# Attention over two long K/V caches on one core: cache loads of 8 MB in 64 KB runs, worked on in place

## The chip, the cores and the metric

The kernel runs on one core of one Trainium2 chip; the other cores are idle. The metric is the device time of one execution in microseconds (us), as a median over several executions. Repeated executions of the kernel before agree within about 0.1% (the widest set is 828.7 to 830.0 us), so differences of 1 us between medians can be seen. The cache lies in HBM, the chip's main memory; sixteen DMA engines copy it to the on-chip memory. The profile of a run spans from its first to its last instruction and is some 1.8 us shorter than the time.

## The reference

There are two independent problems, A and B, of the same shape: one query row, 32 heads of 128 numbers, a cache of 16,384 keys per head in bfloat16. A attends to all keys, B only to the last 4,096.

```python
def _A_ref(x, k_cache, v_cache, wq, wo):          # x: [1, 1, 512]
    q = (x @ wq)  # -> 32 heads of 128
    scores = einsum("bhqd,bhkd->bhqk", q, k) * (Dh ** -0.5)
    p = softmax(scores); o = einsum("bhqk,bhkd->bhqd", p, v)
    return o.reshape(1, 1, 32 * 128) @ wo
# _B_ref: the same with k, v = k_cache[:, :, -4096:, :], v_cache[:, :, -4096:, :]
# result: concatenate([a, b], axis=-1)
```

The inputs that must be read once: 134 MB each of A's K and V, 34 MB each of B's K and V, and 4 MB each of two `wq` and two `wo`: 352 MB in all. (MB in this text are the units of the profile; the "4 MB" of a load are 4,194,304 bytes.)

## The kernel before

Each partition of on-chip memory holds a stretch of keys of one head. A "unit" is one 4 MB load of K and one of V: one head of A (128 partitions x 128 keys, a contiguous run of 32 KB per partition), or four heads of B (32 partitions each, again 128 keys and 32 KB). K and V have two such buffers each.

```python
def _load_kv(nc, cx, unit, which):
    t = pool.tile([P, unit.keys, DH], BF16, tag=tag, name=tag)     # 128 keys: 32 KB per partition
    ...
    n = len(unit.heads)                                            # A: 1, B: 4
    src = view[unit.heads[0] : unit.heads[0] + n].rearrange("g (i l) d -> i g l d", i=P // n)
    cx.o(nc.sync.dma_start(out=t[:, :, :], in_=src[:, 0, :, :] if n == 1 else src))
```

The work on K goes in chunks of 64 keys: VectorE multiplies K by q (broadcast over keys) into a buffer `prod`, adds the upper half of the 128 products to the lower half into a buffer `half`; TensorE, with an identity as weights, sums eight slices of `half` into `red`; VectorE sums the last eight numbers, ScalarE takes the exponentials. TensorE then multiplies V by these ("PV").

```python
def _mult(...):  tensor_tensor(out=ch.prod, in0=u.kt[:, k0:k0+64, :], in1=q.broadcast, op=mult)
def _add(...):   tensor_tensor(out=ch.half, in0=ch.prod[:, :, 0:64], in1=ch.prod[:, :, 64:128], op=add)
...
    cx.kt_pool = pool("kt", 2);  cx.vt_pool = pool("vt", 2)
    cx.prod_pool = pool("prod", 1);  cx.half_pool = pool("half", 2)
```

All loads are issued by SyncE in a fixed order (K of unit i, V of unit i-1, K of unit i+1, ...), each as soon as its buffer is free. `wo` comes last, in pieces that get smaller.

The softmax here doesn't subtract the row's maximum and nothing guards it: scores larger than these inputs give would overflow.

## Time and profile before

| | |
|---|---|
| time, median | 829.0 us |
| bytes moved, mean rate | 352.68 MB, 426 GB/s |
| busy: DMA / VectorE / TensorE / ScalarE | 99% / 71% / 49% / 8% |

The page of the kernel before, cut to the load of the DMA engines, the critical chain, the costly groups and the loads. The rows "DMA" and "GB/s" are the span in 40 equal slices of 20.7 us; the lines with "|" are groups of instructions (count, total busy us, mean ns, then idle time before them and who ended it); the last lines give the time from issue to landing of a load.

```profile
span 827.4 us, 5697 instructions
DMA  9999999999999999999999999999999999999996
GB/s 380 434 430 432 432 432 435 431 432 430 434 429 434 430 431 430 434 431 426 434 432 430 429 431 430 431 432 432 432 430 431 429 431 433 431 433 431 432 423 285
DMA packets 13133, 352.68 MB, mean 426 GB/s; under 512 B 1714, under 2 KB 1716, under 8 KB 2100
...
DMA 69%; DVE 20%; issue 10%; SPq 0%; DVEq 0%; PE 0%
...
L160 DVE TENSOR_TENSOR prod<-kt,qallA 128x8192 bf16<-128x8192 bf16 x64 | 283.3, 4426 | 159.8 <-DMA kt<-in_A_k_cache_dram 159.1
L172 DVE TENSOR_TENSOR half<-prod 128x4096 bf16<-128x4096 bf16 x80 | 182.6, 2282 | 0.0
...
vt<-in_A_v_cache_dram SPq DMA_DIRECT2D x32, 4096.0 KB, 29.6
kt<-in_B_k_cache_dram SPq DMA_DIRECT2D x8, 4096.0 KB, 27.0
```

The slices are flat at 429 to 435 GB/s from the second to the last but one, save two (426 and 423): the stream of the cache is the kernel, and the compute hides under it. VectorE waits 159 us for A's K. The issues in turn wait for VectorE to free a K buffer, as the waits of SyncE show:

```profile
SPq L153 <- DVE prod L160: 428.9, 37, 11.8
```

But the DMA engines don't run dry by it. A V load lands 29.6 us after its issue, though at 432 GB/s its own 4 MB take only 9.7 us: some 20 us of other loads lie in the queue ahead of it. That is the depth of the queue which keeps the engines fed. ("Queue" in this text is the work that has been issued and not yet moved, in us.)

### The profile page before, as it was taken

How to read it: one execution, taken by the hardware profiler on the slowest of the kernel's cores; microseconds unless marked ns; L12 is line 12 of the kernel's file. 1: busy time of each engine (PE TensorE's matmuls, PEld its weight loads, DVE VectorE, ACT ScalarE, POOL GpSimd, SP SyncE). 2: the span in 40 equal slices, each digit the busy share in tenths (PEclk: the TensorE clock that was granted, in tenths of full speed). 3: DMA queues.
4: the chain of work that ended last, by engine and by line, in shares of the span. 5: the costliest groups of instructions: out<-in, count | busy, mean ns of one | idle time of the engine just before them, and what ended most of it. 6: DMA issues, size and time to landing. Idle time of an engine off the chain costs nothing.

```text
span 827.4 us, 5697 instructions
## 1 busy us (share of the span) xinstructions
PE 402.1 (49%) x2368; PEld 139.4 (17%) x2368; DVE 584.8 (71%) x286; ACT 68.2 (8%) x301; POOL 4.6 (1%) x17
## 2 busy tenths in 40 slices
PE   3356434434554535544454445545455345464355
PEld 1112111111211112211121111111112111121123
DVE  2892777777777777766777777777777776777760
ACT  2000011000100001000110001100010000100010
POOL 2000000000000000000000000000000000000000
PEclk9778687666676676776677676666676766766778
DMA  9999999999999999999999999999999999999996
GB/s 380 434 430 432 432 432 435 431 432 430 434 429 434 430 431 430 434 431 426 434 432 430 429 431 430 431 432 432 432 430 431 429 431 433 431 433 431 432 423 285
DMA packets 13133, 352.68 MB, mean 426 GB/s; under 512 B 1714, under 2 KB 1716, under 8 KB 2100
## 3 DMA queue, kind: packets, MB, share of 16 engines
q1 hardware_dynamic: 12820, 352.33, 99.1%
q8 instruction: 18, 0.29, 0.1%
q10 hardware_dynamic: 288, 0.00, 0.0%
q14 instruction: 7, 0.06, 0.0%
HBM read 352.32 MB, written 0.00 MB: 426 GB/s over the span
## 4 chain that ended last, share of the span: by engine, by line
DMA 69%; DVE 20%; issue 10%; SPq 0%; DVEq 0%; PE 0%
DMA kt<-in_A_k_cache_dram 53%; DMA kt<-in_B_k_cache_dram 13%; DVE prod L160 12%; DVE half L172 6%; DMA woB<-in_B_wo_dram 3%; DVE sc L202 2%; SPq L141 0%; DVE recip L266 0%; DVEq L160 0%; PE out L302 0%; SPq L107 0%; DVE rowB L311 0%
## 5 line engine op out<-in xcount | busy, mean ns | idle before, releaser
L185 PE MATMUL red<-half,ident 128*128 128x512 bf16 x640 | 252.4, 566 | 388.7 <-DVE half L172 388.7
L160 DVE TENSOR_TENSOR prod<-kt,qallA 128x8192 bf16<-128x8192 bf16 x64 | 283.3, 4426 | 159.8 <-DMA kt<-in_A_k_cache_dram 159.1
L172 DVE TENSOR_TENSOR half<-prod 128x4096 bf16<-128x4096 bf16 x80 | 182.6, 2282 | 0.0
L185 PEld LDWEIGHTS <-ident 128*128 128x128 bf16 x640 | 81.9, 128 | 534.0 <-issue 506.2
L160 DVE TENSOR_TENSOR prod<-kt,qallB 128x8192 bf16<-128x8192 bf16 x16 | 70.8, 4426 | 40.2 <-DMA kt<-in_B_k_cache_dram 39.9
L232 PE MATMUL acc<-vt,pA 128*16 128x512 bf16 x1024 | 87.2, 474 | 2.0 <-DMA vt<-in_A_v_cache_dram 2.0
L209 ACT ACTIVATE pA<-sc 128x64 bf16<-128x64 f32 x64 | 16.4, 256 | 512.2 <-DVE sc L202 512.2
L202 DVE TENSOR_REDUCE sc<-red 128x64 f32<-128x512 f32 x80 | 54.8, 684 | 3.7 <-PE red L185 3.6
L232 PEld LDWEIGHTS <-pA 128*16 128x16 bf16 x1024 | 22.5, 99 | 72.6 <-issue 65.2
L209 ACT ACTIVATE p_sb<-sc,off 128x64 bf16<-128x64 f32 x64 | 21.5, 336 | 91.4 <-DVE sc L202 91.4
L256 PE MATMUL f_ps<-acc_sb,sel 128*4 128x128 f32 x128 | 16.6, 273 | 10.7 <-ACT acc_sb L243 10.7
L232 PE MATMUL acc<-vt,p_sb 128*16 128x512 bf16 x256 | 21.3, 464 | 0.0
L243 ACT COPY acc_sb<-acc 128x512 f32<-128x512 f32 x16 | 9.4, 586 | 85.6 <-PE acc L232 85.6
L123 PE MATMUL q_ps<-wq_t,xbA 128*128 128x512 bf16 x32 | 8.7, 439 | 13.1 <-DMA wq_t<-in_A_wq_dram 13.1
L256 PEld LDWEIGHTS f_ps<-acc_sb,sel 128*4 128x4 f32 x128 | 9.8, 86 | 14.5 <-ACT acc_sb L243 12.3
L209 ACT ACTIVATION_READ_ACCUMULATOR pA<-sc 128x1 f32 x64 | 11.9, 187 | 0.0
L209 ACT ACTIVATION_READ_ACCUMULATOR p_sb<-sc,off 128x1 f32 x64 | 11.9, 186 | 0.0
L232 PEld LDWEIGHTS <-p_sb 128*16 128x16 bf16 x256 | 5.6, 97 | 16.3 <-issue 14.1
L123 PE MATMUL q_ps<-wq_t,xbB 128*128 128x512 bf16 x32 | 7.2, 378 | 2.0 <-DMA wq_t<-in_B_wq_dram 1.3
L268 ACT ACTIVATE orow<-f_ps,recip 4x128 bf16<-4x128 f32 x16 | 5.7, 358 | 20.5 <-DVE recip L266 20.5
L95 DVE COPY xbB<-xTB 128x32 bf16<-128x32 bf16 x16 | 1.5, 197 | 8.1 <-DMA xTB<-in_B_x_dram 8.1
L266 DVE RECIPROCAL recip<-f_ps 4x1 f32<-4x1 f32 x16 | 2.4, 150 | 5.8 <-PE f_ps L256 5.8
(35 smaller groups left out, 54.8 us busy)
## 6 DMA issues: line engine op xcount, KB each, us to landing
kt<-in_A_k_cache_dram SPq DMA_DIRECT2D x32, 4096.0 KB, 27.0
vt<-in_A_v_cache_dram SPq DMA_DIRECT2D x32, 4096.0 KB, 29.6
kt<-in_B_k_cache_dram SPq DMA_DIRECT2D x8, 4096.0 KB, 27.0
vt<-in_B_v_cache_dram SPq DMA_DIRECT2D x8, 4096.0 KB, 29.6
wq_t<-in_A_wq_dram SPq DMA_DIRECT2D x1, 4096.0 KB, 12.3
wq_t<-in_B_wq_dram SPq DMA_DIRECT2D x1, 4096.0 KB, 24.1
woA<-in_A_wo_dram SPq DMA_DIRECT2D x2, 2048.0 KB, 31.3
woB<-in_B_wo_dram SPq DMA_DIRECT2D x1, 2048.0 KB, 23.8
```

Of the source, the lines that this page charges most:

```text
L95: cx.o(nc.vector.tensor_copy(st.xb[:, c, g, :].rearrange("p (i r) -> p r i", r=R)[:, g, :], xT[:, c : c + 1].broadcast_to([P, P // R]),))
L123: cx.o(nc.tensor.matmul(q_ps[:, :], lhsT=st.xb[:, c, g, :], rhs=w[:, g, j * (512 // DH) : (j + 1) * (512 // DH), :], start=(g == 0 and c = ...
L160: cx.o(nc.vector.tensor_tensor(out=ch.prod[:, :, :], in0=u.kt[:, ch.k0 : ch.k0 + U, :], in1=q.rearrange("p (o d) -> p o d", o=1).broadcast ...
L172: cx.o(nc.vector.tensor_tensor(out=ch.half[:, :, :], in0=ch.prod[:, :, 0 : DH // 2], in1=ch.prod[:, :, DH // 2 : DH], op=ALU.add,))
L185: cx.o(nc.tensor.matmul(ch.red[:, :, :], lhsT=cx.ident[:, :], rhs=ch.half[:, :, b * W : (b + 1) * W], start=(b == 0), stop=(b == nb - 1),))
L202: cx.o(nc.vector.tensor_reduce(out=sc[:, :], in_=ch.red[:, :, :], axis=AX.X, op=ALU.add))
L209: cx.o(nc.scalar.activation(out=ch.p[:, :, g, :], in_=sc[:, :].rearrange("p (t e) -> p t e", e=4), func=ACT.Exp, scale=SCALE, bias=0.0 if ...
L232: cx.o(nc.tensor.matmul(gr.acc[r : r + 4 * G, :], lhsT=ch.p[:, t, :, :], rhs=u.vt[:, k : k + 4, :], start=(first and t < 4), stop=(last an ...
L243: cx.o(nc.scalar.copy(gr.acc_sb[:, :], gr.acc[:, :]))
L256: cx.o(nc.tensor.matmul(gr.f_ps[:, 0:DH], lhsT=cx.sel[:, e, :], rhs=gr.acc_sb[:, e * DH : (e + 1) * DH], start=False, stop=(e == 3), skip_ ...
L266: cx.o(nc.vector.reciprocal(recip[:, :], gr.f_ps[:, DH : DH + 1]))
L268: cx.o(nc.scalar.activation(out=gr.orow[:, :], in_=gr.f_ps[:, 0:DH], func=ACT.Copy, scale=recip[:, 0:1]))
```

## The change

Fewer, longer descriptors (a descriptor here is one contiguous run that a DMA engine moves; the trace has one packet for each: 8,192 of A's packets have 32 KB before, 4,096 have 64 KB after): K/V buffers of 8 MB, 64 KB per partition. A's load takes two heads, interleaved on the partitions, in runs of 64 KB. B's load takes eight heads as two transfers of four heads each, still in runs of 32 KB. To make room, the products and half sums are written over K itself, and V has one buffer instead of two. The diff, cut to its core:

```diff
-G = 4
+KEYS = 256
 def _load_kv(...):
-    t = pool.tile([P, unit.keys, DH], BF16, tag=tag, name=tag)
-    src = view[unit.heads[0] : unit.heads[0] + n].rearrange("g (i l) d -> i g l d", i=P // n)
-    cx.o(nc.sync.dma_start(out=t[:, :, :], in_=src[:, 0, :, :] if n == 1 else src))
+    t = pool.tile([P, KEYS, DH], BF16, tag=tag, name=which)
+    for u in load.units:                       # A: 1 unit of 2 heads; B: 2 units of 4 heads
+        src = view[u.h0 : u.h0 + u.R].rearrange("g (i l) d -> i g l d", l=st.keys)
+        cx.o(nc.sync.dma_start(out=t[:, u.k0 : u.k0 + st.keys, :], in_=src))
 def _mult(...):
-    out=ch.prod[:, :, :], in0=u.kt[:, ch.k0 : ch.k0 + U, :],
+    out=k, in0=k,
 def _add(...):
-    out=ch.half[:, :, :], in0=ch.prod[:, :, 0 : DH // 2], in1=ch.prod[:, :, DH // 2 : DH],
+    out=k[:, :, 0 : DH // 2], in0=k[:, :, 0 : DH // 2], in1=k[:, :, DH // 2 : DH],
-    cx.vt_pool = pool("vt", 2)
-    cx.prod_pool = pool("prod", 1);  cx.half_pool = pool("half", 2)
+    cx.vt_pool = pool("vt", 1)
+    st.R, st.keys = (2, KEYS) if name == "A" else (4, KEYS // 2)
 # order of work, load i of 20, chunk c of 4:
+            if i and c == min(i - 1, 2):
+                pv(loads[i - 1])
 ... (both wq are loaded first, into the V buffer; wo at the end into it; masks,
      sums of the exponentials and the last steps are adapted to two or four heads per unit)
```

More of the change, by code (lines that the diff above doesn't have):

```diff
@@ L41, with __init__ @@
 class _Loads:
-    def __init__(self):
-        self.todo, self.free = [], {}
+    def __init__(self, free):
+        self.todo, self.free = [], free
     def add(self, pool, fn):
@@ L60, in pump, with __init__ @@
             fn()
-class _Group:
-    def __init__(self, st, i):
-        self.st, self.i, self.heads = st, i, list(range(i * G, (i + 1) * G))
-        self.acc = self.cs = None
 class _Chunk:
     def __init__(self, unit, i):
-        self.unit, self.i, self.k0 = unit, i, i * U
-        self.last_of_unit = self.k0 + U == unit.keys
+        self.unit, self.i, self.k0 = unit, i, unit.k0 + i * U
 class _Unit:
-    kt = vt = None
-def _load_x(nc, cx, st):
+    def __init__(self, st, i, load, k0):
+        self.st, self.i, self.R = st, i, st.R
+        self.load, self.k0 = load, k0
+        self.h0 = i * st.R
+        self.chunks = [_Chunk(self, c) for c in range(st.keys // U)]
+        self.stage = None
@@ L85, in _load_x, with __init__ @@
+class _Load:
+    def __init__(self, st, i):
+        self.st = st
+        n = KEYS // st.keys
+        self.units = [_Unit(st, i * n + j, self, j * st.keys) for j in range(n)]
+        self.chunks = [ch for u in self.units for ch in u.chunks]
+def _load_x(nc, cx, st, at):
     D = st.wq.shape[0]
     KC = D // P
+    R = st.R
     xT = cx.singles.tile([P, KC], BF16, tag=f"xT{st.name}", name=f"xT{st.name}")
     nc.scalar.dma_start(out=xT[:, :], in_=st.x[0, 0, :].rearrange("(p c) -> p c", c=KC))
-    R = st.mix
@@ L90, in _load_x @@
-    st.xb = cx.singles.tile([P, KC, R, P], BF16, tag=f"xb{st.name}", name=f"xb{st.name}")
-    if R > 1:
-        cx.o(nc.vector.memset(st.xb[:, :, :, :], 0.0))
+    n = KC * R * P
+    st.xb = cx.scr[:, at : at + n].rearrange("p (c g m) -> p c g m", c=KC, g=R)
+    cx.o(nc.vector.memset(cx.scr[:, at : at + n], 0.0))
     for g in range(R):
-        for c in range(KC):
-            cx.o(nc.vector.tensor_copy(
-                st.xb[:, c, g, :].rearrange("p (i r) -> p r i", r=R)[:, g, :],
-                xT[:, c : c + 1].broadcast_to([P, P // R]),
-            ))
@@ L101, in _load_wq @@
-def _load_wq(nc, cx, st, tag):
+        cx.o(nc.vector.tensor_copy(
+            st.xb[:, :, g, :].rearrange("p c (i r) -> p r c i", r=R)[:, g, :, :],
+            xT[:, :].rearrange("p (c o) -> p c o", o=1).broadcast_to([P, KC, P // R]),
+        ))
+    return at + n
+def _load_wq(nc, cx, st, w):
     D, N = st.wq.shape
     KC = D // P
-    st.wq_tag = tag
-    pool = cx.kt_pool if tag == "kt" else cx.vt_pool
-    st.wq_t = pool.tile([P, KC, N], BF16, tag=tag, name="wq_t")
-    cx.o(nc.sync.dma_start(out=st.wq_t[:, :, :], in_=st.wq.rearrange("(p c) f -> p c f", c=KC)))
+    if w == 0:
+        cx.wq_t = cx.vt_pool.tile([P, 2, KC, N], BF16, tag="vt", name="wq_t")
+    st.wq_t = cx.wq_t[:, w, :, :]
+    cx.o(nc.sync.dma_start(out=st.wq_t, in_=st.wq.rearrange("(p c) f -> p c f", c=KC)))
@@ L114, in _q @@
     KC = D // P
-    R = st.mix
+    R = st.R
     n = N // R
@@ L130, in _q, with _load_kv @@
         cx.o(nc.scalar.copy(st.qall[:, j * 512 : (j + 1) * 512], q_ps[:, :]))
-    cx.loads.release(st.wq_tag)
 def _load_wo(nc, cx, st, j0, n):
     J = st.wo.shape[0] // P
-    if j0 == 0:
-        st.wo_t = cx.kt_pool.tile([P, J, st.DN], BF16, tag="kt", name=f"wo{st.name}")
+    if cx.wo_t is None:
+        cx.wo_t = cx.vt_pool.tile([P, 2, J, st.DN], BF16, tag="vt", name="wo_t")
     src = st.wo.rearrange("(p j) f -> p j f", j=J)
+    st.wo_t = cx.wo_t[:, st.at // st.DN, :, :]
     cx.o(nc.sync.dma_start(out=st.wo_t[:, j0 : j0 + n, :], in_=src[:, j0 : j0 + n, :]))
-def _load_kv(nc, cx, unit, which):
-    pool, tag = (cx.kt_pool, "kt") if which == "k" else (cx.vt_pool, "vt")
-    t = pool.tile([P, unit.keys, DH], BF16, tag=tag, name=tag)
-    setattr(unit, tag, t)
-    st = unit.st
-    view = st.k_view if which == "k" else st.v_view
-    n = len(unit.heads)
-    src = view[unit.heads[0] : unit.heads[0] + n].rearrange("g (i l) d -> i g l d", i=P // n)
-    cx.o(nc.sync.dma_start(out=t[:, :, :], in_=src[:, 0, :, :] if n == 1 else src))
+def _load_kv(nc, cx, load, which, tag):
+    pool = cx.kt_pool if tag == "kt" else cx.vt_pool
+    t = pool.tile([P, KEYS, DH], BF16, tag=tag, name=which)
+    setattr(load, which, t)
+    load.v_tag = tag
+    st = load.st
+    view = st.k_view if which == "kt" else st.v_view
+    for u in load.units:
+        src = view[u.h0 : u.h0 + u.R].rearrange("g (i l) d -> i g l d", l=st.keys)
+        cx.o(nc.sync.dma_start(out=t[:, u.k0 : u.k0 + st.keys, :], in_=src))
 def _mult(nc, cx, ch):
     u = ch.unit
-    ch.prod = cx.prod_pool.tile([P, U, DH], BF16, tag="prod", name="prod")
-    q = u.st.qall[:, u.q_at * DH : (u.q_at + 1) * DH]
+    k = u.load.kt[:, ch.k0 : ch.k0 + U, :]
+    q = u.st.qall[:, u.i * DH : (u.i + 1) * DH]
     cx.o(nc.vector.tensor_tensor(
-        out=ch.prod[:, :, :],
-        in0=u.kt[:, ch.k0 : ch.k0 + U, :],
+        out=k, in0=k,
         in1=q.rearrange("p (o d) -> p o d", o=1).broadcast_to([P, U, DH]),
@@ L165, in _mult @@
     ))
-    if ch.last_of_unit:
-        cx.loads.release("kt")
 def _add(nc, cx, ch):
-    ch.half = cx.half_pool.tile([P, U, DH // 2], BF16, tag="half", name="half")
+    k = ch.unit.load.kt[:, ch.k0 : ch.k0 + U, :]
     cx.o(nc.vector.tensor_tensor(
-        out=ch.half[:, :, :],
-        in0=ch.prod[:, :, 0 : DH // 2],
-        in1=ch.prod[:, :, DH // 2 : DH],
-        op=ALU.add,
+        out=k[:, :, 0 : DH // 2], in0=k[:, :, 0 : DH // 2], in1=k[:, :, DH // 2 : DH], op=ALU.add,
     ))
@@ L187, in _red @@
             lhsT=cx.ident[:, :],
-            rhs=ch.half[:, :, b * W : (b + 1) * W],
+            rhs=ch.unit.load.kt[:, ch.k0 : ch.k0 + U, b * W : (b + 1) * W],
             start=(b == 0),
@@ L191, in _red @@
         ))
+    if ch is ch.unit.load.chunks[-1]:
+        cx.loads.release("kt")
 def _softmax(nc, cx, ch):
-    u, gr = ch.unit, ch.unit.group
-    if gr.cs is None:
-        gr.cs = cx.cs_pool.tile([P, 2, G], F32, tag=f"cs{gr.st.name}", name="cs")
-    sc = cx.small.tile([P, U], F32, tag="sc", name="sc")
-    cx.o(nc.vector.tensor_reduce(out=sc[:, :], in_=ch.red[:, :, :], axis=AX.X, op=ALU.add))
-    if len(u.heads) == 1:
-        ch.p = cx.pA[u.heads[0] % G][ch.i]
-    else:
-        ch.p = cx.p_pool.tile([P, U // 4, G, 4], BF16, tag="p", name="p_sb")
-    for h in u.heads:
-        g = h % G
+    u = ch.unit
+    R = u.R
+    if ch.i == 0:
+        u.cs = cx.cs_pool.tile([P, len(u.chunks), R], F32, tag=f"cs{u.st.name}", name="cs")
+    sc = cx.sc_pool.tile([P, U], F32, tag="sc", name="sc")
+    cx.o(nc.vector.tensor_reduce(out=sc[:, :], in_=ch.red[:, :, :], axis=AX.X, op=ALU.add))
+    ch.p = u.st.p_pool.tile([P, U // 4, R, 4], BF16, tag=f"p{u.st.name}", name="p_sb")
+    for g in range(R):
         cx.o(nc.scalar.activation(
@@ L213, in _softmax @@
             scale=SCALE,
-            bias=0.0 if len(u.heads) == 1 else cx.off[:, g : g + 1],
-            accum_out=gr.cs[:, ch.i, g : g + 1],
-        ))
-def _pv(nc, cx, ch):
-    u, gr = ch.unit, ch.unit.group
-    first = u.heads[0] == gr.heads[0] and ch.i == 0
-    last = u.heads[-1] == gr.heads[-1] and ch.last_of_unit
-    if first:
-        cx.turn = 1 - cx.turn
-        gr.acc = cx.acc[cx.turn]
-    T = U // 4
+            bias=u.st.off[:, g : g + 1],
+            accum_out=u.cs[:, ch.i, g : g + 1],
+        ))
@@ L229, in _pv @@
+def _pv(nc, cx, u):
+    R = u.R
+    u.csum = cx.small.tile([P, R], F32, tag=f"csum{u.st.name}", name="csum")
+    cx.o(nc.vector.tensor_reduce(
+        out=u.csum[:, :], in_=u.cs[:, :, :].rearrange("p i g -> p g i"), axis=AX.X, op=ALU.add,
+    ))
+    cx.turn = 1 - cx.turn
+    acc = cx.acc[cx.turn]
+    T = u.st.keys // 4
     for t in range(T):
         r = 32 * (t % 4)
-        k = ch.k0 + 4 * t
+        ch, k = u.chunks[4 * t // U], u.k0 + 4 * t
         cx.o(nc.tensor.matmul(
-            gr.acc[r : r + 4 * G, :],
-            lhsT=ch.p[:, t, :, :],
-            rhs=u.vt[:, k : k + 4, :],
-            start=(first and t < 4),
-            stop=(last and t >= T - 4),
-        ))
@@ L239, in _pv @@
-    if ch.last_of_unit:
-        cx.loads.release("vt")
-    if last:
-        gr.acc_sb = cx.accs_pool.tile([P, 4 * DH], F32, tag="accs", name="acc_sb")
-        cx.o(nc.scalar.copy(gr.acc_sb[:, :], gr.acc[:, :]))
-    return gr if last else None
-def _fin_fold(nc, cx, gr):
-    gr.f_ps = cx.psf_pool.tile([G, DH + 1], F32, tag="f", name="f_ps")
-    for i in range(2):
-        cx.o(nc.tensor.matmul(
-            gr.f_ps[:, DH : DH + 1], lhsT=gr.cs[:, i, :], rhs=cx.ones_col[:, 0:1],
-            start=(i == 0), stop=(i == 1), skip_group_check=True,
-        ))
+            acc[r : r + 4 * R, :],
@@ new lines, in _pv, with _fin_fold @@
+            lhsT=ch.p[:, t % (U // 4), :, :],
+            rhs=u.load.vt[:, k : k + 4, :],
+            start=(t < 4),
+            stop=(t >= T - 4),
+        ))
+    if u is u.load.units[-1]:
+        cx.loads.release(u.load.v_tag)
+    u.acc_sb = cx.accs_pool.tile([P, 4 * DH], F32, tag="accs", name="acc_sb")
+    cx.o(nc.scalar.copy(u.acc_sb[:, :], acc[:, :]))
+def _fin_fold(nc, cx, u):
+    R = u.R
+    u.f_ps = cx.psf_pool.tile([8, DH + 1], F32, tag="f", name="f_ps")
+    cx.o(nc.tensor.matmul(
+        u.f_ps[0:R, DH : DH + 1], lhsT=u.csum[:, :], rhs=cx.ones_col[:, 0:1],
+        start=True, stop=True, skip_group_check=True,
+    ))
@@ L255, in _fin_fold, with _fin_row @@
     for e in range(4):
         cx.o(nc.tensor.matmul(
-            gr.f_ps[:, 0:DH],
-            lhsT=cx.sel[:, e, :],
-            rhs=gr.acc_sb[:, e * DH : (e + 1) * DH],
+            u.f_ps[0:R, 0:DH],
+            lhsT=cx.sel[:, e, 0:R],
+            rhs=u.acc_sb[:, e * DH : (e + 1) * DH],
             start=False, stop=(e == 3), skip_group_check=True,
         ))
-def _fin_row(nc, cx, gr):
-    recip = cx.small.tile([G, 1], F32, tag="recip", name="recip")
-    cx.o(nc.vector.reciprocal(recip[:, :], gr.f_ps[:, DH : DH + 1]))
-    gr.orow = cx.small.tile([G, DH], BF16, tag="orow", name="orow")
+def _fin_row(nc, cx, u):
+    R = u.R
+    recip = cx.small.tile([8, 1], F32, tag="recip", name="recip")
+    cx.o(nc.vector.reciprocal(recip[0:R, :], u.f_ps[0:R, DH : DH + 1]))
+    u.orow = cx.small.tile([8, DH], BF16, tag="orow", name="orow")
@@ L268, in _fin_row, with _fin_col @@
     cx.o(nc.scalar.activation(
-        out=gr.orow[:, :], in_=gr.f_ps[:, 0:DH], func=ACT.Copy, scale=recip[:, 0:1]
+        out=u.orow[0:R, :], in_=u.f_ps[0:R, 0:DH], func=ACT.Copy, scale=recip[0:R, 0:1]
     ))
-def _fin_col(nc, cx, gr):
-    st = gr.st
+def _fin_col(nc, cx, u):
+    st = u.st
     J = st.wo.shape[0] // P
-    R = DH // J
-    at = (len(st.groups) - 1 - gr.i) * G * R
-    for r in range(R):
+    n = DH // J
+    last = u.i == len(st.units) - 1
+    for r in range(n):
+        at = cx.place_at - n * u.h0 - r
@@ L281, in _fin_col @@
         cx.o(nc.tensor.matmul(
             cx.oc_ps[:, st.oc_at : st.oc_at + J],
-            lhsT=cx.place[0:G, r, at : at + P],
-            rhs=gr.orow[:, r * J : (r + 1) * J],
-            start=(cx.oc_first and r == 0), stop=(gr.i == len(st.groups) - 1 and r == R - 1),
+            lhsT=cx.place[0 : u.R, at : at + P],
+            rhs=u.orow[0 : u.R, r * J : (r + 1) * J],
+            start=(cx.oc_first and r == 0), stop=(last and r == n - 1),
             skip_group_check=True,
@@ L309, in _out @@
     if j0 + n == J:
-        row = cx.singles.tile([1, st.DN], BF16, tag=f"row{st.name}", name=f"row{st.name}")
+        row = cx.accs_pool.tile([1, st.DN], BF16, tag="accs", name=f"row{st.name}")
         cx.o(nc.vector.tensor_copy(row[0:1, 0:w], out[0]))
@@ L342 @@
     cx.singles = pool("singles", 1)
-    cx.small = pool("small", 4)
+    cx.small = pool("small", 1)
     cx.kt_pool = pool("kt", 2)
-    cx.vt_pool = pool("vt", 2)
-    cx.prod_pool = pool("prod", 1)
-    cx.half_pool = pool("half", 2)
-    cx.accs_pool = pool("accs", 2)
+    cx.vt_pool = pool("vt", 1)
+    cx.accs_pool = pool("accs", 1)
     cx.cs_pool = pool("cs", 2)
-    cx.p_pool = pool("p", 4)
+    cx.sc_pool = pool("sc", 2)
+    cx.p_poolA = pool("pA", 8)
+    cx.p_poolB = pool("pB", 4)
     cx.red_pool = pool("red", 2, **PS)
@@ L354, with problem @@
     cx.psout_pool = pool("psout", 1, **PS)
-    ld = cx.loads = _Loads()
-    ld.free = {"kt": 2, "vt": 2}
+    ld = cx.loads = _Loads({"kt": 1, "vt": 1})
+    cx.scr = cx.kt_pool.tile([P, KEYS * DH], BF16, tag="kt", name="scr")
+    cx.wo_t = None
+    def problem(name, x, k_cache, v_cache, wq, wo, sk0, W, at):
+        st = _Problem()
+        st.name, st.x, st.wq, st.wo, st.at = name, x, wq, wo, at
+        st.R, st.keys = (2, KEYS) if name == "A" else (4, KEYS // 2)
+        assert st.R * W == P * st.keys
+        st.DN = wo.shape[1]
+        st.k_view = k_cache[0, :, sk0 : sk0 + W, :]
+        st.v_view = v_cache[0, :, sk0 : sk0 + W, :]
+        st.oc_at, st.out_rows = (0, (0, 32)) if name == "A" else (64, (64, 96))
+        st.p_pool = cx.p_poolA if name == "A" else cx.p_poolB
+        n = KEYS // st.keys * st.R
+        st.loads = [_Load(st, i) for i in range(k_cache.shape[1] // n)]
+        st.units = [u for x in st.loads for u in x.units]
+        return st
@@ new lines @@
+    stA = problem("A", A_x, A_k_cache, A_v_cache, A_wq, A_wo, 0, SkA, 0)
+    stB = problem("B", B_x, B_k_cache, B_v_cache, B_wq, B_wo, SkB - WB, WB, A_wo.shape[1])
+    loads = []
+    per = len(stA.loads) // len(stB.loads)
+    for i, x in enumerate(stA.loads):
+        loads.append(x)
+        if i % per == per - 1:
+            loads.append(stB.loads[i // per])
+    ld.add("vt", lambda: _load_wq(nc, cx, stA, 0))
+    ld.add(None, lambda: _load_wq(nc, cx, stB, 1))
+    for i, x in enumerate(loads):
+        ld.add("kt", lambda x=x: _load_kv(nc, cx, x, "kt", "kt"))
+        if i:
+            ld.add("vt", lambda x=loads[i - 1]: _load_kv(nc, cx, x, "vt", "vt"))
@@ L358 @@
+    ld.add("kt", lambda x=loads[-1]: _load_kv(nc, cx, x, "vt", "kt"))
+    J = A_wo.shape[0] // P
+    pieces = [(stA, 0, J // 2), (stA, J // 2, J // 2)]
+    j0 = 0
+    for x in (J // 2, J // 4, J // 8, J // 16, J // 16):
+        pieces.append((stB, j0, x))
+        j0 += x
+    for i, p in enumerate(pieces):
+        ld.add(None if i else "vt", lambda p=p: _load_wo(nc, cx, *p))
+    ld.pump()
+    at = _load_x(nc, cx, stA, 0)
+    at = _load_x(nc, cx, stB, at)
     cx.ones_col = cx.singles.tile([P, 1], F32, tag="ones_col", name="ones_col")
@@ L359 @@
     nc.gpsimd.memset(cx.ones_col[:, :], 1.0)
-    ones_mat = cx.singles.tile([P, P], BF16, tag="ones_mat", name="ones_mat")
-    nc.gpsimd.memset(ones_mat[:, :], 1.0)
+    ones = cx.scr[:, at : at + 2 * P]
+    nc.gpsimd.memset(ones, 1.0)
     cx.ident = cx.singles.tile([P, P], BF16, tag="ident", name="ident")
@@ L364 @@
         out=cx.ident[:, :],
-        in_=ones_mat[:, :],
+        in_=ones[:, 0:P],
         pattern=[[-1, P]],
@@ L371 @@
     )
-    cx.sel = cx.singles.tile([P, 4, G], F32, tag="sel", name="sel")
+    n_r = DH // J
+    cx.place_at = n_r * (stA.units[-1].h0) + n_r - 1
+    w = cx.place_at + P
+    cx.place = cx.singles.tile([8, 2 * P], BF16, tag="place", name="place")
+    nc.gpsimd.affine_select(
+        out=cx.place[:, 0:w],
+        in_=ones[0:8, 0:w],
+        pattern=[[1, w]],
+        compare_op=ALU.is_equal,
+        fill=0.0,
+        base=-cx.place_at,
+        channel_multiplier=-n_r,
+    )
+    cx.sel = cx.singles.tile([P, 4, 8], F32, tag="sel", name="sel")
     nc.vector.tensor_reduce(
         out=cx.sel[:, :, :].rearrange("p e g -> p g e"),
-        in_=cx.ident[:, :].rearrange("p (t g e) -> p g e t", t=4, g=8)[:, 0:G, :, :],
+        in_=cx.ident[:, :].rearrange("p (t g e) -> p g e t", t=4, g=8),
         axis=AX.X,
@@ L381 @@
     )
-    cx.off = cx.singles.tile([P, G], F32, tag="off", name="off")
-    nc.vector.tensor_reduce(
-        out=cx.off[:, :],
-        in_=cx.ident[:, :].rearrange("p (i g) -> p g i", g=G),
-        axis=AX.X,
-        op=ALU.add,
-    )
-    nc.vector.tensor_scalar(
-        out=cx.off[:, :], in0=cx.off[:, :], scalar1=-1.0, scalar2=1000.0,
-        op0=ALU.add, op1=ALU.mult,
-    )
-    J = A_wo.shape[0] // P
-    R = DH // J
-    w = 2 * P - G * R
-    ones_row = cx.singles.tile([G, R * w], BF16, tag="ones_row", name="ones_row")
-    nc.gpsimd.memset(ones_row[:, :], 1.0)
-    cx.place = cx.singles.tile([G, R, w], BF16, tag="place", name="place")
-    nc.gpsimd.affine_select(
-        out=cx.place[:, :, :],
-        in_=ones_row[:, :].rearrange("p (r c) -> p r c", r=R),
-        pattern=[[-1, R], [1, w]],
-        compare_op=ALU.is_equal,
-        fill=0.0,
-        base=-(P - G * R),
-        channel_multiplier=-R,
-    )
-    cx.pA = []
-    for g in range(G):
-        cx.pA.append([])
-        for i in range(2):
-            t = cx.singles.tile([P, U // 4, G, 4], BF16, tag=f"pA{g}{i}", name=f"pA{g}{i}")
-            nc.gpsimd.memset(t[:, :, :, :], 0.0)
-            cx.pA[g].append(t)
+    for st in (stA, stB):
+        st.off = cx.singles.tile([P, st.R], F32, tag=f"off{st.name}", name=f"off{st.name}")
+        nc.vector.tensor_reduce(
+            out=st.off[:, :],
+            in_=cx.ident[:, :].rearrange("p (i g) -> p g i", g=st.R),
+            axis=AX.X,
+            op=ALU.add,
+        )
+        nc.vector.tensor_scalar(
+            out=st.off[:, :], in0=st.off[:, :], scalar1=-1.0, scalar2=1000.0,
+            op0=ALU.add, op1=ALU.mult,
+        )
     cx.turn = 0
@@ L427 @@
     ]
-    def problem(name, x, k_cache, v_cache, wq, wo, sk0, W, at):
-        st = _Problem()
-        st.name, st.x, st.wq, st.wo, st.W, st.at = name, x, wq, wo, W, at
-        st.H = k_cache.shape[1]
-        st.DN = wo.shape[1]
-        st.k_view = k_cache[0, :, sk0 : sk0 + W, :]
-        st.v_view = v_cache[0, :, sk0 : sk0 + W, :]
-        st.oc_at, st.out_rows = (0, (0, 32)) if name == "A" else (64, (64, 96))
-        st.mix = 1 if W == SkA else G
-        st.groups = [_Group(st, i) for i in range(st.H // G)]
-        return st
@@ L441 @@
-    stA = problem("A", A_x, A_k_cache, A_v_cache, A_wq, A_wo, 0, SkA, 0)
-    stB = problem("B", B_x, B_k_cache, B_v_cache, B_wq, B_wo, SkB - WB, WB, A_wo.shape[1])
-    units = []
-    for h in range(stA.H):
-        units.append((stA, [h]))
-        if h % G == G - 1:
-            units.append((stB, list(range(h - G + 1, h + 1))))
-    chunks = []
-    for i, (st, heads) in enumerate(units):
-        u = units[i] = _Unit()
-        u.st, u.heads, u.group = st, heads, st.groups[heads[0] // G]
-        u.keys = st.W * len(heads) // P
-        u.q_at = heads[0] // len(heads)
-        u.chunks = [_Chunk(u, i) for i in range(u.keys // U)]
-        chunks += u.chunks
@@ L460 @@
-    ld.add("vt", lambda: _load_wq(nc, cx, stA, "vt"))
-    n = len(units)
-    for i in range(n + 1):
-        if i == G - 1:
-            ld.add("kt", lambda: _load_wq(nc, cx, stB, "kt"))
-        if i < n:
-            ld.add("kt", lambda u=units[i]: _load_kv(nc, cx, u, "k"))
-        if i:
-            ld.add("vt", lambda u=units[i - 1]: _load_kv(nc, cx, u, "v"))
-    pieces = [(stA, 0, J // 2), (stA, J // 2, J // 2)]
-    j0 = 0
-    for x in (J // 2, J // 4, J // 8, J // 16, J // 16):
-        pieces.append((stB, j0, x))
-        j0 += x
@@ L474 @@
-    for p in pieces:
-        ld.add(None if p[1] else "kt", lambda p=p: _load_wo(nc, cx, *p))
-    _load_x(nc, cx, stA)
-    _load_x(nc, cx, stB)
-    ld.pump()
     _q(nc, cx, stA)
+    _q(nc, cx, stB)
+    ld.release("kt")
+    ld.release("vt")
     fins = []
     def fin_pe():
-        for gr in fins:
-            if gr.stage == 0:
-                _fin_fold(nc, cx, gr)
-                gr.stage = 1
-            elif gr.stage == 2:
-                _fin_col(nc, cx, gr)
-                gr.stage = 9
-        fins[:] = [gr for gr in fins if gr.stage != 9]
@@ L494, in fin_dve @@
-    def fin_dve():
-        for gr in fins:
-            if gr.stage == 1:
-                _fin_row(nc, cx, gr)
-                gr.stage = 2
-    def pv(ch):
-        gr = _pv(nc, cx, ch)
-        if gr is not None:
-            gr.stage = 0
-            fins.append(gr)
-    prev = None
-    waiting = []
-    for c, ch in enumerate(chunks):
-        if c == 2 * (G - 1):
-            _q(nc, cx, stB)
-        _mult(nc, cx, ch)
-        if prev is not None:
-            _softmax(nc, cx, prev)
-            waiting.append(prev)
-        fin_pe()
-        _add(nc, cx, ch)
-        fin_dve()
-        _red(nc, cx, ch)
-        if len(waiting) > 1:
-            pv(waiting.pop(0))
-        prev = ch
@@ L522 @@
-    _softmax(nc, cx, prev)
-    waiting.append(prev)
-    for ch in waiting:
-        fin_pe()
-        fin_dve()
-        pv(ch)
+        for u in fins:
+            if u.stage == 0:
+                _fin_fold(nc, cx, u)
+                u.stage = 1
+            elif u.stage == 2:
+                _fin_col(nc, cx, u)
+                u.stage = 9
+        fins[:] = [u for u in fins if u.stage != 9]
+    def fin_dve():
+        for u in fins:
+            if u.stage == 1:
+                _fin_row(nc, cx, u)
+                u.stage = 2
@@ new lines, in pv @@
+    def pv(load):
+        for u in load.units:
+            fin_pe()
+            fin_dve()
+            _pv(nc, cx, u)
+            u.stage = 0
+            fins.append(u)
+    prev = None
+    for i, x in enumerate(loads):
+        for c, ch in enumerate(x.chunks):
+            _mult(nc, cx, ch)
+            if prev is not None:
+                _softmax(nc, cx, prev)
+            fin_pe()
+            _add(nc, cx, ch)
+            fin_dve()
+            _red(nc, cx, ch)
+            if i and c == min(i - 1, 2):
+                pv(loads[i - 1])
+            prev = ch
@@ L528 @@
+    _softmax(nc, cx, prev)
+    fin_pe()
+    fin_dve()
+    pv(loads[-1])
     while fins:
```

## The prediction

> **What bounds the kernel now.** The cache stream. The page moves 352 MB in 827.4 us, on average 426 GB/s; its slices show a DMA busy share of 90% or more until the last one, and 429 to 435 GB/s in nearly all. In the chain of waits DMA is 69%; the piece "DMA kt" comes again every 38.85 us, in which two 4 MB K and two 4 MB V loads pass: 9.71 us per load, 432 GB/s. VectorE is busy 71%, TensorE 49%; VectorE idles 199 us before the multiply, waiting for K. What is not stream is some 2.5 us at the start and 7 us at the end (819 to 827 us in the windows: the DMA engines run dry one by one, the last wo pieces land, the row goes out).
>
> **What the change does.**
> - Bytes: all stay. A's 268 MB come in 64 KB runs instead of 32 KB; B's 67 MB stay at 32 KB.
> - A 4 MB load is 8 descriptors for each of 16 engines, 1.214 us each. [...] A saves 256 descriptors per engine[...].
> - Interleaved heads: B's loads do this already, and the issue list has the same landing time for K of A and B (27.0 us): no cost.
> - VectorE: the same elements, in place: multiplies of 4.43 us, half sums of 2.28, reductions of 0.68. I expect these times again. An 8 MB load needs 4 x 7.4 = 30 us of VectorE in a period of 38.8. A's exponentials double in number; ScalarE is at 8%.
> - Buffering: V of load i goes out only when PV of load i-1 is done, after the third chunk of load i: 22 + 3.6 + 4.2 = 30 us after that K landed. The K transfer ahead of it ends at 38.8 us, so 8 to 9 us of queue are left (before: some 20 us). Tighter, but not dry.
> - Start: both wq first (8 MB), then an 8 MB K; q ends near 31 us, then the next K is issued, and the queue lasts to about 42 us. The end stays as it is.
>
> **On the critical path:** only the stream's rate, 2 to 3 us, and jitter of 2 us either way.
>
> **Prediction:** 826.5 us, 821.5 to 831.5 us for 8 in 10. Faster by over 2%: 0.02; within 2%: 0.93; slower by over 2%: 0.05.
>
> **What would show it right:** slices of 432 to 435 GB/s without holes; about 4,100 DMA packets fewer; a period of 38.7 to 38.8 us per 8 MB pair of K and V; issue to landing of V near 28 us (19.4 of its own, 8 to 9 of queue); multiply and half sum at 4.43 and 2.28 us.
>
> **What would make it wrong:** 64 KB runs slower than 32 KB ones (slices under 425 GB/s in A's stretches only)[...]; holes in the slices, where the single V buffer lets the queue run dry (landing of V near 20 us); VectorE slower in place (a half sum near 4.5 us would give 40 us per load and make VectorE the limit); a start in which q ends after 42 us.

The sum on record came to 826.5 us, 2.5 us below the 829.0 us of the kernel before; its terms for the gain (the loss per descriptor, what A's 256 fewer descriptors per engine save, and the most to be had) are cut, so it can't be added up from what is left. The engines running dry at the end show as DMA shares of 0.65 from 819 us, 0.17 from 822 and 0.00 from 824 in the windows of the kernel before.

## The result

The changed kernel takes 826.54 us (826.41 to 826.56, four runs); the kernel before, on the same chip, 829.0 us. The ratio is 0.997 (95% interval 0.9955 to 0.9984). Ratios here are the mean time of one kernel's runs over that of the other's of the same rounds, so not quite the ratio of the medians quoted. Executions over 1.5% slower than the fastest of the same kernel are left out of the means. The same lines of the page as before, after the change:

```profile
span 824.8 us, 5931 instructions
DMA  9999999999999999999999999999999999999997
GB/s 381 432 458 408 454 411 452 416 446 436 416 454 417 449 420 443 429 428 443 415 444 429 433 432 432 436 418 448 423 424 438 445 418 448 417 429 436 427 423 293
DMA packets 8527, 352.71 MB, mean 428 GB/s; under 512 B 1202, under 2 KB 1204, under 8 KB 1588
...
DMA 57%; DVE 24%; PE 13%; issue 4%; ACT 1%; another core or an unknown queue 1%; SPq 0%; ACTq 0%; DVEq 0%
DMA kt<-in_A_k_cache_dram 43%; DVE kt L163 13%; DVE kt L172 9%; DMA vt<-in_A_v_cache_dram 7%; PE red L182 6%; PE acc L226 6%; DMA vt<-in_B_v_cache_dram 4%; DMA wo_t<-in_B_wo_dram 4%; DVE sc L200 2%; PE f_ps L247 1%; ACT acc_sb L236 1%; SPq L112 0%; PE out L292 0%; DVE rowB L301 0%
...
L163 DVE TENSOR_TENSOR kt<-kt,qallA 128x8192 bf16<-128x8192 bf16 x64 | 282.7, 4417 | 118.1 <-DMA kt<-in_A_k_cache_dram 118.1
L172 DVE TENSOR_TENSOR kt<-kt 128x4096 bf16<-128x4096 bf16 x80 | 182.2, 2278 | 0.0
...
kt<-in_A_k_cache_dram SPq DMA_DIRECT2D x16, 44.4
vt<-in_A_v_cache_dram SPq DMA_DIRECT2D x16, 29.2
```

There are 4,606 packets fewer: 4,096 data packets of A and 512 tiny ones because there are 32 loads fewer, less two that don't belong to the loads. Writing in place costs VectorE nothing (4,417 and 2,278 ns against 4,426 and 2,282). V's time to landing is about the same number as before, but now 19.4 us of it are V's own 8 MB. So less than 10 us of queue are left where there were 20, and TensorE has come into the critical chain (13%, before 0%). About half of it is PV ("acc", 6%), which V's next load waits for. Another 6% is the sum "red": as it now reads K's own buffer, the buffer is free only after it, and no longer after the multiply. The chain shows what it hangs from; the flat 9s of the DMA row show that the engines never ran dry.

The slices now scatter from 408 to 458 GB/s. That is not a stream with holes: over the stretch from 100 to 780 us the windows of the two kernels read as follows (window, its length, busy us and counts by engine, granted clock, DMA share, GB/s), before first:

```profile
100.00:780.00 680.00, 328.30 (x1902) 110.24 (x1895) 506.29 (x224) 52.86 (x252) 0.00 (x0) 0.70 1.00 431
```

```profile
100.00:780.00 680.00, 329.84 (x1944) 122.12 (x1944) 517.86 (x257) 82.34 (x384) 0.00 (x0) 0.67 1.00 432
```

The experiment "a32_perm" below, with the same transfers into the same buffers but in packets of 32 KB, has flat slices again, 429 to 436 from the second to the 38th:

```profile
GB/s 380 434 431 430 436 429 430 433 432 433 434 431 432 430 429 432 431 430 433 430 430 431 430 431 433 432 431 429 432 433 431 429 432 433 430 433 431 430 424 291
```

So the scatter goes with the 64 KB packets, and it lies in the counting: the slices book a packet whole where it starts, and 16 packets of 64 KB are 1 MB, an eighth of a slice. With each packet's bytes spread over its own duration (worked out from the packet records), the changed kernel's slices are flat too, at 431 to 434 GB/s from the second to the 38th (the kernel before: 429 to 433).

The trace also holds each DMA packet's duration. Its median and mean by size, from the profiled runs (not a view of the page; worked out from the packet records; 8,192 bytes and those under 2,048 left out):

```
bytes     count   median ns  mean ns            count   median ns  mean ns
          (before)                              (after)
 2048       256       84       85.8               256       84       85.0
 4096       128      159      160.7               128      159      160.4
16384       402      613      637.2               403      614      636.4
32768     10496     1215     1218.3              2304     1215     1221.2
65536         -        -         -               4096     2420     2424.2
```

A second 32 KB costs 2,420 - 1,215 = 1,205 ns, which is 27.19 GB/s per engine, 435.1 GB/s for sixteen. What is left of a packet's time is nearly the same at every size of the table: 1,215 - 1,205 = 10 ns, and 8 to 11 ns for the others at the same rate. The sum of all packet times divided by 16 engines fell from 821.7 to 818.6 us, 3.0 us, where the kernel gained 2.5. The trace alone thus suggests a fixed cost per descriptor. It doesn't prove it, because the order at the start, the number of transfers and the buffers changed as well.

### The profile page after: what moved, and what is told of

Read it like the earlier page. It is cut to its first block, busy times and chain, and to the rows that moved or that the text cites. A ratio compares the mean times of both kernels' runs of the same rounds, so it can differ in the third digit from the quotient of the medians.

```text
span 824.8 us, 5931 instructions
## 1 busy us (share of the span) xinstructions
PE 400.4 (49%) x2448; PEld 152.1 (18%) x2448; DVE 583.0 (71%) x307; ACT 98.8 (12%) x441; POOL 1.2 (0%) x8
## 4 chain that ended last, share of the span: by engine, by line
DMA 57%; DVE 24%; PE 13%; issue 4%; ACT 1%; another core or an unknown queue 1%; SPq 0%; ACTq 0%; DVEq 0%
DMA kt<-in_A_k_cache_dram 43%; DVE kt L163 13%; DVE kt L172 9%; DMA vt<-in_A_v_cache_dram 7%; PE red L182 6%; PE acc L226 6%; DMA vt<-in_B_v_cache_dram 4%; DMA wo_t<-in_B_wo_dram 4%; DVE sc L200 2%; PE f_ps L247 1%; ACT acc_sb L236 1%; SPq L112 0%; PE out L292 0%; DVE rowB L301 0%
## 5 line engine op out<-in xcount | busy, mean ns | idle before, releaser
L182 PE MATMUL red<-kt,ident 128*128 128x512 bf16 x640 | 254.5, 569 | 370.6 <-DVE kt L172 370.6
L163 DVE TENSOR_TENSOR kt<-kt,qallA 128x8192 bf16<-128x8192 bf16 x64 | 282.7, 4417 | 118.1 <-DMA kt<-in_A_k_cache_dram 118.1
L172 DVE TENSOR_TENSOR kt<-kt 128x4096 bf16<-128x4096 bf16 x80 | 182.2, 2278 | 0.0
L226 PE MATMUL acc<-vt,p_sb 128*8 128x512 bf16 (+1 forms) x1280 | 93.3, 450 | 15.6 <-DMA vt<-in_A_v_cache_dram 10.0
L203 ACT ACTIVATE p_sb<-sc,offA 128x64 bf16<-128x64 f32 x128 | 43.5, 341 | 368.3 <-DVE sc L200 368.3
L163 DVE TENSOR_TENSOR kt<-kt,qallB 128x8192 bf16<-128x8192 bf16 x16 | 70.4, 4402 | 0.0
L226 PEld LDWEIGHTS <-p_sb 128*8 128x8 bf16 (+1 forms) x1280 | 34.9, 98 | 77.6 <-issue 57.7
L203 ACT ACTIVATE p_sb<-sc,offB 128x64 bf16<-128x64 f32 x64 | 21.5, 337 | 99.9 <-DVE sc L200 99.9
L247 PE MATMUL f_ps<-acc_sb,sel 128*2 128x128 f32 (+1 forms) x192 | 24.9, 272 | 16.3 <-ACT acc_sb L236 16.3
L203 ACT ACTIVATION_READ_ACCUMULATOR p_sb<-sc,offA 128x1 f32 x128 | 24.0, 187 | 0.0
L127 PE MATMUL q_ps<-wq_t,scr 128*128 128x512 bf16 x64 | 15.9, 411 | 14.2 <-DMA wq_t<-in_A_wq_dram 13.2
```

What stands on the lines that cost most here:

```text
L127: cx.o(nc.tensor.matmul(q_ps[:, :], lhsT=st.xb[:, c, g, :], rhs=w[:, g, j * (512 // DH) : (j + 1) * (512 // DH), :], start=(g == 0 and c = ...
L163: cx.o(nc.vector.tensor_tensor(out=k, in0=k, in1=q.rearrange("p (o d) -> p o d", o=1).broadcast_to([P, U, DH]), op=ALU.mult,))
L172: cx.o(nc.vector.tensor_tensor(out=k[:, :, 0 : DH // 2], in0=k[:, :, 0 : DH // 2], in1=k[:, :, DH // 2 : DH], op=ALU.add,))
L182: cx.o(nc.tensor.matmul(ch.red[:, :, :], lhsT=cx.ident[:, :], rhs=ch.unit.load.kt[:, ch.k0 : ch.k0 + U, b * W : (b + 1) * W], start=(b == ...
L203: cx.o(nc.scalar.activation(out=ch.p[:, :, g, :], in_=sc[:, :].rearrange("p (t e) -> p t e", e=4), func=ACT.Exp, scale=SCALE, bias=u.st.of ...
L226: cx.o(nc.tensor.matmul(acc[r : r + 4 * R, :], lhsT=ch.p[:, t % (U // 4), :, :], rhs=u.load.vt[:, k : k + 4, :], start=(t < 4), stop=(t >= ...
```

## The experiments

The main theory: the kernel is its DMA stream; a descriptor costs about 10 ns beside its bytes; nothing else in the change matters as long as the queue never empties. The rival: the gain comes from the rest of the change (start, fewer and larger transfers, one V buffer), and the descriptors are a coincidence. Each experiment was run beside the kernel before on the same chip.

### The number of descriptors (after_again, a32_perm, a8_perm, before_a16)

The softmax and the weighted sum don't depend on the order of the keys, as long as K and V have the same order. So a partition's keys may come from several places of the head. The load stays one transfer of 8 MB into the same buffer at the same point in the order, and only the number of runs changes (2 for a32_perm, 8 for a8_perm):

```diff
-        src = view[...].rearrange("g (i l) d -> i g l d", l=st.keys)
+        src = view[...].rearrange("g (h i l) d -> i g h l d", h=2, l=st.keys // 2)     # A only
```

The changed kernel again, as the reference of the set:

> The changed kernel once more, as the reference of this set on this chip. Both theories: 826.5 us, 0.997 of the kernel before.

It took 826.43 us (826.35 to 826.83, five runs), ratio 0.997.

> A's loads stay one transfer of 8 MB into the same buffers in the same order, but each partition's 256 keys come as two runs of 32 KB from two places of the head (the softmax and the sum don't depend on the order of keys). Theory 1, a fixed cost of about 10 ns per descriptor: 256 more descriptors on each DMA engine, +2.6 us against the changed kernel, 829.1 us, the time of the kernel before. Theory 2, the gain came from the rest of the change (the order at the start, fewer and larger transfers, one V buffer): 826.5 us.

It took 828.84 us (828.75 to 829.12), ratio to the kernel before 0.9999, interval 0.9986 to 1.0012. With 32 KB runs the changed kernel is as fast as the kernel before (828.96 in this set): all of the gain is gone, and all the rest of the change, taken together, is worth about 0.1 us (by the interval, no more than about 1 us either way). The rival is out as the cause of the gain.

> As the run with two runs of 32 KB, but eight runs of 8 KB per partition. Theory 1: 1792 more descriptors on each engine at 10.3 ns, +18.5 us, 845 us. Theory 2: within 1 us of 826.5 us. A third possibility, that it is the address pattern and not the number of descriptors, would give a step that does not grow with the number: 829 us here as well.

It took 843.48 us, 17.05 us more than the changed kernel of the same set. Per descriptor: 17.05 us / 1,792 = 9.5 ns, and for a32_perm 2.41 us / 256 = 9.4 ns. So the cost grows with the number and is not a step that an address pattern makes. My 18.5 us came from 10.3 ns, within the 8 to 11 ns of the packet table, and was a little high.

The same in the kernel before, where A's 32 KB runs become two of 16 KB, with the 4 MB loads and the two V buffers left alone:

> The kernel before, with A's 32 KB runs cut into two of 16 KB (keys permuted, result the same): 4 MB loads and two V buffers stay. Fixed cost per descriptor (9.4 ns as measured): 512 more on each engine, +4.8 us, 833.8 us, 1.0058. If the cost belonged to the 8 MB kernel alone: 829 us.

It took 833.93 us (the kernel before in this set: 829.08), ratio 1.0057; 4.85 us / 512 = 9.5 ns. The cost belongs to the descriptor, not to one of the two kernels.

### B in longer runs too (b64)

If 64 KB are good for A, B could have them: eight heads, 16 partitions each. The kernel's helpers allow it with one edit:

```diff
-        st.R, st.keys = (2, KEYS) if name == "A" else (4, KEYS // 2)
+        st.R, st.keys = (2, KEYS) if name == "A" else (8, KEYS)
```

> B too in 64 KB runs: eight heads interleaved on the partitions, one 8 MB transfer in place of two of 4 MB. Theory 1: 64 descriptors per engine fewer at 10.3 ns, -0.7 us, 825.9 us. Theory 2 gives no more than 0.3 us. ScalarE gets 8 exponentials per chunk of B (4.2 us of a chunk of 7.3 us): if that holds up the PV behind the single V buffer, the time rises instead.

It took 1,024.6 us (1,010 to 1,084 in six runs, three of them slow; ratio 1.2274). Both theories were far off, and the time rose for another reason than the exponentials. The profiled run counts as slow (1,038 us of span), but a few per cent are not the question here: the slices (lines of its page), and two windows, the first in a stretch of B and the second in a stretch of A:

```profile
GB/s 404 444 427 422 440 440 210 263 425 263 217 430 437 430 432 278 215 402 318 205 342 442 427 432 371 200 268 434 205 205 429 430 432 430 270 213 318 202 205 231
L163 DVE TENSOR_TENSOR kt<-kt,qallB 128x8192 bf16<-128x8192 bf16 x16 | 70.7, 4416 | 135.0 <-DMA kt<-in_B_k_cache_dram 135.0
```

```profile
171.00:200.00 29.00, 1.97 (x12) 0.75 (x10) 0.13 (x1) 0.36 (x1) 0.00 (x0) 0.58 1.01 213
341.00:371.00 30.00, 12.89 (x52) 4.16 (x56) 27.29 (x13) 2.31 (x12) 0.00 (x0) 0.51 0.99 428
```

The DMA share is 1.01 in B's stretch, so all engines are busy, yet they move half as much. The packet records say the same: 64 KB take a median of 5.1 us in the first window and 2.42 us in the second. Compute is not what is waited for: ScalarE is nearly idle in that window, and VectorE waits 135 us for B's K.

### Why B was slow (a_x8, a_x4, a_x8_far)

In B's load the outer dimension of the transfer now has 16 steps of 8 places, in the changed kernel 32 of 4 (B) and 64 of 2 (A). Two theories: the places in on-chip memory, or the addresses in HBM. The mechanism for the first is not shown by any trace or run here. Its forecast: 16 steps of 8 places are slow as in b64, from whatever addresses, and 32 of 4 run as B does in the changed kernel. A's load can be given these forms without B, without more heads and without more exponentials: two adjacent heads are 128 blocks of 64 KB in one row. (The edit is shown simplified; B's load stays as it was.)

```diff
-        src = view[...].rearrange("g (i l) d -> i g l d", l=st.keys)            # 64 steps x 2 places
+        src = view.rearrange("g s d -> (g s) d")[u.h0 * st.W : (u.h0 + u.R) * st.W]
+        src = src.rearrange("(x i l) d -> i x l d", x=8, l=st.keys)             # 16 x 8 (a_x4: x=4, 32 x 4)
... (masks and the copies of x follow: head = place // 4)
```

> Why was B in 64 KB runs slow (205 GB/s in B's stretches)? Here B is as in the changed kernel, and A's 8 MB loads take the same 128 blocks of 64 KB of the same two adjacent heads, but in the order 16 outer steps x 8 places (partition = 8 x step + place; block = 16 x place + step) instead of 64 x 2. No more heads, no more exponentials. [...] A's stretches fall to about 205 to 215 GB/s, 64 KB packets at about 5.1 us, the whole near 1450 us. Rivals: eight heads 4 MB apart in HBM, or the exponentials for eight heads hold things up: then this stays within 10 us of 826.5.

> The same with 32 outer steps x 4 places. [...] as B with four heads in the changed kernel: 826.5 us, 1 us more or less. If the distance of the jumps in HBM matters (2 MB here, 4 MB in the changed kernel, 1 MB in the run with 8 places), this lies clearly above 826.5 us.

a_x8 took 1,506 us in the one profiled (the only other run, 1,563 us, was slow); a_x4 took 826.54 us (ratio 0.9969). The slices of a_x8, and a window in a stretch of A:

```profile
GB/s 331 199 210 209 204 215 195 220 311 215 230 286 216 197 218 200 219 236 289 206 318 210 215 207 220 215 218 309 216 200 317 212 211 213 213 210 213 307 284 268
```

```profile
220.00:240.00 20.00, 8.84 (x86) 3.65 (x86) 6.08 (x4) 2.39 (x10) 0.00 (x0) 0.73 1.01 210
```

With 16 outer steps A falls to 200 to 220 GB/s in most slices (the higher ones hold B's loads too), and the median 64 KB packet takes 5.07 us; with 32 steps the time is that of the changed kernel. So it is neither B nor the number of heads. The jumps in HBM don't explain it either: 1 MB (a_x8) and 4 MB (b64) are slow, 2 MB (a_x4) and 4 MB (the changed kernel) are fast. One difference in addresses remained: if each engine takes one step, which no run shows, both slow runs read 16 neighbouring blocks at one time. In a_x8_far, partition p reads block p, so that neighbouring partitions read neighbouring addresses; only the form of the transfer stays 16 x 8.

```diff
+            src = flat[at : at + 16 * n].rearrange("(i x l) d -> i x l d", i=16, l=st.keys)
+            src = bass.AP(tensor=src.tensor, offset=src.offset, ap=[(src.ap[0][0] - DH, 16)] + list(src.ap[1:]))
```

> Wrong result on purpose (the heads get mixed); only the transfers matter. As the slow run with 16 outer steps x 8 places in A, into the same partitions, but from other addresses: block = 8 x step + place, the outer step 256 B short of 512 KB so that the two dimensions stay apart. [...] it is as slow: 64 KB packets near 5.1 us, 200 to 220 GB/s in A's stretches, near 1500 us. Rival (16 neighbouring blocks of 64 KB read at one time are slow in HBM): [...] packets near 2.42 us, near 827 us.

It took 1,525 us (one run; relative error 0.28); the median 64 KB packet took 5.08 us. Its output is wrong, which doesn't matter for the time. Outer steps 512 KB apart instead of 64 KB help nothing. What is shown: 16 outer steps of 8 partitions halve the rate (200 to 220 GB/s instead of 432), in A and in B and with all three orders of addresses that were tried; 32 x 4 and 64 x 2 don't. In all these orders the blocks of steps and places lie 64 KB, 512 KB (less 256 B) or 1 to 4 MB apart; that some such spacing in HBM plays a part is less likely after a_x8_far, but other spacings were not tried. That the places in on-chip memory are the cause agrees with all these runs, but it was my guess, and no mechanism is shown: the trace doesn't say which engine wrote which partition, and no run shows how the engines share out 16, 32 or 64 steps.

### How much queue the single V buffer leaves (pv_late, pv_early, before_v1)

> PV of load i-1 after the fourth chunk of load i instead of the third, so the next V is issued 7.3 us later. In the changed kernel V's time from issue to landing is 29.2 us, 19.4 of its own, so 9.8 us of queue were left. My theory (the single V buffer is free as long as the queue is not empty): 2 to 3 us of queue are left, V lands about 22 us after issue, the time is 826.5 to 829 us. Rival (less depth of queue costs by itself[...]): over 5 us more.

```diff
-            if i and c == min(i - 1, 2):
+            if i and c == min(i - 1, 3):        # pv_early: 1
```

pv_late took 839.17 us, 12.7 us more. By the figures it was the rival that was met (over 5 us more), and mine was wrong. But what was lost was lost to an empty queue, as my theory has it; whether depth has a value of its own is left to pv_early. Its slices, and three windows around the issue of a V load at 256.7 us:

```profile
DMA  9999999999998999999998999999999899999997
GB/s 386 464 400 448 450 405 445 421 436 436 425 441 351 450 414 438 405 447 401 430 456 366 445 403 450 398 407 448 439 411 449 357 451 442 410 401 447 419 419 319
```

```profile
252.00:254.00 2.00, 1.27 (x24) 0.53 (x13) 0.00 (x0) 0.59 (x1) 0.00 (x0) 0.93 0.68 295
254.00:256.00 2.00, 2.00 (x38) 1.62 (x37) 0.22 (x2) 0.36 (x1) 0.00 (x0) 1.00 0.04 8
256.00:258.00 2.00, 1.56 (x21) 0.87 (x14) 1.32 (x1) 0.59 (x1) 0.00 (x0) 1.00 0.11 33
```

The DMA share falls to 0.04: the queue ran dry. Counted from the packet records, without the first 20 and the last 25 us of the span, the engines stood idle for 10.8 us each on average (0.1 in the changed kernel), so 10.7 of the 13.4 us by which the two profiled spans differ. Longer packets make up the rest: 64 KB took 2,440 ns on average, not 2,424, some 4 us for an engine's 256. Two things were wrong in my sum. First, I took V's own 19.4 us off its time to landing; but a V load that meets an empty queue lands after 22.2 us here, not after 19.4; its first packet starts 1.3 us after the issue. Second, I took the median; single loads of A's V in the changed kernel land after 26.4 to 29.8 us in the steady part. So 4 to 7.5 us of queue are left, not 9.8, and moving PV by 7.3 us eats it.

> PV of load i-1 after the second chunk of load i instead of the third. The smallest time from issue to landing of a V load was 22.5 us in the changed kernel (3 us of queue left) and 19.8 us with PV after the fourth chunk (dry). Theory: as long as no load finds the queue empty, its depth is worth nothing: the same 826.5 us within 0.5 us, smallest time to landing 26 to 30 us, though TensorE now waits longer for V to land. Rival: depth of queue has a value of its own, then 1 us or more is gained.

pv_early took 826.58 us, ratio 0.9972: the time of the changed kernel. (The "22.5 us" of the text above was misread: it is the first half of one of B's V loads, 4 MB, and stays at 22.5 here. A's 8 MB loads land after 33 to 36 us, where I expected 26 to 30.) TensorE waits longer for V, as its wait in the two kernels shows, changed kernel first:

```profile
  DMA vt<-in_A_v_cache_dram: 10.0, 6
  DMA vt<-in_B_v_cache_dram: 5.6, 1
```

```profile
  DMA vt<-in_A_v_cache_dram: 44.1, 16
```

B's V is not waited for any more. The 28.5 us that TensorE waits more cost nothing, and 5 to 7 us more of queue gain nothing. In these runs depth of queue is worth nothing until it is gone.

Last, the one part of the change that could hurt, alone: one V buffer in the kernel before.

```diff
-    cx.vt_pool = pool("vt", 2);  ld.free = {"kt": 2, "vt": 2}
+    cx.vt_pool = pool("vt", 1);  ld.free = {"kt": 2, "vt": 1}
```

> The kernel before with one V buffer in place of two, nothing else: this part of the change alone. V of unit i then waits for PV of unit i-1 instead of i-2, one period of 19.4 us later; V landed 29.6 us after issue, 9.7 of its own and 19.9 of queue, so 0.5 us of queue would be left, less than a transfer takes to begin. Theory: a hole of 1 to 2 us in each of 40 units, 870 to 910 us. If the depth of queue had no part in it: 829 us.

(The time to begin, as measured: in the kernel before, the first 32 KB packet starts 1.24 us after the first load's issue at 0.80 us; in pv_late it was 1.3 us.)

It took 896.9 us, ratio 1.0834, within the expected range. Its slices, and V's issues to landing, with those of the kernel before first:

```profile
DMA to landing us min/median/max: 28.1/29.6/40.1
```

```profile
vt<-in_A_v_cache_dram SPq DMA_DIRECT2D x32, 4096.0 KB, 13.2
GB/s 396 425 305 435 386 399 415 407 417 405 417 376 400 398 422 393 401 399 418 403 417 386 427 371 408 410 408 374 418 390 388 403 410 408 371 440 368 389 235 328
DMA to landing us min/median/max: 12.0/20.1/24.0
```

The last landing line is of K and V together; V's own lie at 12 to 15 us but for two near the start (median 13.2 for A's), where a 4 MB load needs 9.7 us of its own: nearly every V load finds the queue empty or nearly so. By the packet records, counted as above, the engines stood idle for 51.6 us each (0.2 in the kernel before), 1.3 us for each of the 40 units, and 32 KB took 1,245 ns on average instead of 1,218, which is another 18 us; the profiled spans differ by 67.4 us. Why one V buffer is affordable in the changed kernel is argued, not shown: its loads are twice as long, so that a K transfer of 19.4 us is still running while PV frees V. No run changed the length of the loads alone.

No version beat the changed kernel.

## Why the prediction was right

- **The bound: right.** The stream was and is the kernel. ScalarE's busy time rose from 68 to 99 us, TensorE's and VectorE's stayed within 2 us (402 to 400 and 585 to 583), and none of it shows in the time.
- **The gain of 2 to 3 us: right, size included.** The traces bear the size out: the packets show 10 ns per descriptor, the runs 9.4 to 9.5 ns, and a32_perm takes the gain away again, 2.4 us. An estimate from the median packet times of the kernel before alone would have done: eight of 4 KB take 8 x 159 - 1,215 = 57 ns more than one of 32 KB, two of 16 KB 2 x 613 - 1,215 = 11 ns more, so 8 to 11 ns per descriptor, and 2.1 to 2.8 us for 256. The total of 826.5 us was met within 0.1 us, and that is luck: the 10 ns are a small difference of nearly equal times (2 x 1,215 against 2,420 ns), and the rest of the change happened to be worth about 0.1 us. The range of 821.5 to 831.5 us proves nothing by itself, since it also holds 829.0, no change at all; what bears the prediction out is a32_perm.
- **Interleaved heads cost nothing: right for two and four.** a_x4 shows that four places in A are free as well. The thought behind it ("B does this already") would have been wrong for eight: b64 and a_x8.
- **VectorE in place: right**, within 0.2%.
- **The single V buffer: right in its outcome, off in its size.** I gave 8 to 9 us of queue; the smallest was about 4 us, since single loads land up to 2.8 us before the median, and a load into an empty queue needs 2.8 us more than its bytes. pv_late shows the edge.
- **The signs to look for:** packets down by 4,606, as said about 4,100 of data; V's landing 29.2 us (said: near 28). The slices were said to be 432 to 435 GB/s; as the page books them they scatter between 408 and 458; their mean (432) is as said, and spread over the packets' durations they lie at 431 to 434. The start went as said (q near 31 us): the second K load was issued at 30.2 us. The period of a load pair could not be checked: landings scatter by 1 to 2 us, more than the 0.1 us in question.

## What to carry to other kernels

When a kernel is one long stream, first work out the floor (bytes over the rate that the packets show, here 435 GB/s, plus a constant per descriptor, here about 10 ns); here one packet of 64 KB instead of two of 32 KB saves 10 ns in 2,430, 0.4%, and moving PV earlier (pv_early) added nothing to it. Count the queue in microseconds at its worst load, not at the median, and against the time that a load into an empty queue takes (22.2 us here, with 19.4 of its own); here spare depth cost and gained nothing (pv_early, 826.58 us), and missing depth cost at once (pv_late, 839.17 us). Before you interleave more heads on partitions, look at the outer dimension of the transfer: here 16 steps used all engines (DMA share 1.01) and still halved the rate (210 GB/s in that window instead of 432).
